# Joint half steps for two pairs of heads, f32 P for two pairs of batch 1, unscaled P in batch 0, and the cap in registers

## The chip, the cores and the metric

One core of one Trainium2 chip runs the whole program. The metric is the device time of one execution in microseconds. Five engines work side by side: TensorE (PE: matmuls, with its weight loads shown apart as PEld), VectorE (DVE), ScalarE (ACT), GpSimd (POOL) and SyncE (SP), which here issues the DMAs.

## The reference

Attention with a soft cap for 4 batches of 12 heads, 448 positions of 64 numbers, then a feed-forward layer with a leaky activation on the 1792 tokens:

```python
scores = scale * q @ k.T                       # (4, 12, 448, 448)
scores = cap * tanh(scores / cap)
attn = exp(scores - max(scores)); attn /= sum(attn) + 1e-9
x = (attn @ v)                                 # heads put side by side: 1792 x 768
h = x @ w_in                                   # 768 x 2048
g = maximum(h, 0) + alpha * minimum(h, 0)
out = g @ w_out                                # 2048 x 768
```

`w_in`, `w_out` and `alpha` come as 64-bit floats, which the kernel makes into f32 with integer operations on DVE.

## The kernel before

Products that must be nearly f32-exact are made in one of two ways: as f32 matmuls (each appears as two instructions in the trace), or as f16 matmuls of operands that were split into a high and a low f16 part, three or four products for one.

**Attention** goes by pairs of heads (6 pairs in a batch). The 448 rows of scores of a head are 3 full blocks of 128 rows and 64 more. `steps` takes two blocks at a time, one of each head: a score product in PSUM, tanh on ACT (`L553`), the row maximum on DVE (`L558`), a small operation that makes the bias of it (`L560`), exp on ACT with the row sums (`L565`), `GUARD` and reciprocal on the sums (`L570`, `L573`). The last 64 rows of both heads stand together in one block of 128 rows, and this half step has half as much to do on every engine but the same number of operations. So a pair takes 4 steps in batches 1 to 3. Batch 0 is cut into two parts of 192 and 256 rows: 2 steps for each pair and part, and of the 192-row part one of the two is a half step.

Then P must be turned (its keys put on partitions). In batch 0, `turn_32` (`L600` to `L616`) makes a diagonal matrix of the row factors 1/sum on ACT or POOL and multiplies each 128x112 piece of the block with it in f32 (`L612`), 4 products for a block, 42 blocks in all; PSUM is copied to `ptall`, and `PV_32` (`L665`) multiplies with the raw f32 v. In batches 1 to 3, `turn_split` scales P by the factors, splits it into f16 parts on ACT, DVE and POOL, and DMAs turn it; `PV_split` (`L651`) takes 24 f16 products for a pair.

Scores of batches 0 and 1 are f32 products of 64x128 tiles (`scores_32`, `L528`). For batches 2 and 3, q and k are scaled and split into `nat`, the two parts of a head side by side on 128 columns and k's parts doubled by a copy (`L768`); one DMA turns 24 groups of 112x128, and a score block is 2 products over 128 rows of the array (`L785`).

**Weights**: DVE converts and splits 16 chunks of w_in and 16 of w_out (`wi`, `wp`); `norms` takes a Gram product on PE and its absolute maximum on DVE (`L370`, 8 times).

**The layer**: `mm1` (`L806`) multiplies w_in with x of a batch, `mm2` (`L847`) w_out with g. The first mm2 needs all of w_out and its scales, and mm1 of batch 1 writes over the g that mm2 of batch 0 reads.

**Order**: every operation is recorded with a priority and a model time per engine (`op`), and `Plan.order` lists them by a simulated run of all queues, choosing the engine where several could do an operation (`either`, `diff`: ACT, DVE, POOL). The result is a fixed order per engine. Until a planned time, PE gets dummy products (`fill`, `L1063`) where it would have nothing to do, so that its clock stays up.

Of the kernel before, what the change touches and what calls it, by code (L numbers as in the profile page):

```python
# [10 lines left out]
F32 = mybir.dt.float32  # L11
# [14 lines left out]
PD_A = 6  # L26
PD_B = 6
MQ = 3
AQ = 3
PEN = 4509.92  # L30
PEN2 = -1345.18
PENP = 6482.25
B0_P = -50.35
LD_P = -35.85
LO_P = 301.38
MM_P = 3324.02
X_P = 53.71
ST_P = 19.81
ST1_P = 13.45
PV_P = 374.14  # L40
QK_P = -32.7
V_P = -1.09
WI_P = 40.03
WI_S = -0.97
A_S = 13.05
MM1_P = 198.89
WO_P = 329.05
WO_S = -16.5
WT_P = -1461.61
WT_S = -141.91  # L50
B1_P = 277.05
B_S = 241.79
EVAC_P = -145.66
# [14 lines left out]
QA = 0.5  # L68
VA = 1.0
FS = [0, 6]  # L70
TURN = 95.0
TURN_P = 905.0
SCORE = 1040.0
# [5 lines left out]
OFF = [34.6, 0.4, 29.9, -6.1, 0.0, 1.5, -90.6, 40.5, 0.0, 0.0, -257.7, 0.0, 2.6, -1.0, 26.8, -8.5, -42.6, 107.4, 10.3, 125.2, 8.6, -267.5, -58.1, 2.0, -9.3, 235.7, 4.8, -32.5, 207.0, 194.2, 463.8, 229.6, 0.0, -31.2, -255.6, -6.9, -24.3, 57.8, -178.1, 70.7, 0.0, 225.2, -115.2, -52.7, 0.0, -130.7, 63.2, 240.7, 63.4, -111.4, 0.0, 0.0, 9.4, 97.8, -60.1, -181.2, -100.1, -35.7, 137.8, 0.0, -6.1, -78.0, -257.2, 31.2, -2.2, -147.9, 21.3, -0.4, 0.0, 21.9, 119.4, -148.7, 89.0, -63.5, 14.5, 76.1, -40.7, -49.1, 31.5, -2.8, 125.9, -8.9, 99.3, -23.6, -83.9, 175.4, 11.7, 163.5, -170.9, 0.0, 13.5, 0.2, -5.3, 0.2, -132.0, -577.9, -1.6, 9.7, -185.1, -10.0, 15.0, -245.3, 0.0, -22.7, 32.7, 149.3, -1091.5, -40.3, 0.0, -672.3, 15.6, -127.9, -897.3, 55.4, -59.5, 0.0, 167.9, 2.2, 12.5, -39.1, 123.8, -60.7, -437.0, -54.8, -543.8, -541.5, 4.4, 0.0, -1.4, -92.4, -0.7, -60.4, 150.0, 75.5, -504.3, 26.7, 69.5, 182.6, -11.4, -57.0, 55.8, 95.6, -4.2, 2.6, 230.8, 0.0, -572.4, 62.6, 1.6, -54.4, 0.0, -3.0, 20.2, 99.9, 396.1, 2.6]  # L79
# [9 lines left out]
class Plan:  # L89
# [16 lines left out]
    def op(self, prio, times, fn, r=(), w=(), rows=1.0, port=True):  # L106
        o = lambda: None
        o.prio, o.times, o.fn, o.rows, o.idx, o.port = prio + OFF[self.tag], times, fn, rows, len(self.ops), port
# [24 lines left out]
    def order(self):  # L133
# [8 lines left out]
        port = {"dve": 0.0, "pool": 0.0}  # L142
# [46 lines left out]
        while todo:  # L189
# [10 lines left out]
            for e in free:  # L200
# [3 lines left out]
                while ready[e]:  # L204
# [20 lines left out]
                    elif e == "pe":  # L225
                        free[e] = run_pe(t, o.rows)
# [36 lines left out]
def kernel(  # L263
# [72 lines left out]
    nat = ct([P, 6 * NCH, P], F16, "nat")  # L336
    qkTs = ct([P, 2, 6 * NCH, CP], F16, "qkTs")
    aux = qkTs[:, 1].rearrange("p g t -> p (g t)").bitcast(F32)
    qzs = [aux[:, :512], aux[:, 512:1024]]
    qzr = [(("qkT", 1), 0, 512), (("qkT", 1), 512, 1024)]  # L340
# [3 lines left out]
    diags = ct([P, 4, P], F32, "diags")  # L344
# [4 lines left out]
    ams = ct([P, 3, 8], F32, "ams")  # L349
    vam = ct([P, 2, 2 * NPAIR], F32, "vam")  # L350
# [17 lines left out]

    def absmax(o, i):
        nc.vector.tensor_reduce(out=o, in_=i, axis=AX.X, op=ALU.max, apply_absolute_value=True)  # L370

# [80 lines left out]
    def vslot(b, pair):  # L452
        n = 2 * NCH * D
        if b == 0 and pair < 3:
            return nat.rearrange("p g t -> p (g t)").bitcast(F32)[:CP, pair * n:(pair + 1) * n], ("nat", pair * n, pair * n + n)
        if b == 0 and pair == 5:
            return xring[:CP, 6:].rearrange("p i e t -> p (i e t)").bitcast(F32)[:, :n], ("x", 12 * S, 12 * S + 2 * n)
        return rvs[:CP, pair % 2], ("rv", pair % 2, pair % 2 + 1)
# [33 lines left out]
    def spans(n, c):  # L492
# [4 lines left out]
        else:  # L497
            for h in range(2):
                yield h, slice(h * QP, (h + 1) * QP), slice(n - QP, n)

    step_no = [0]
    xpos = {}

    def xslot(b, pair):
# [603 lines left out]
```

## Time and profile before

| | us |
|---|---|
| median of 3 runs (lowest, highest) | 695.26 (694.31, 695.97) |
| the profiled execution | 696.31 |
| its span, first to last instruction | 694.5 |
| PE busy | 680.4 |
| DVE busy | 486.9 |
| ACT busy | 420.7 |
| POOL busy | 265.0 |

The span is the time between the first and the last instruction on the engines; 1.8 us of the execution lie around it. Busy shares are means over stages with different limits. Matmuls are pipelined, so the length of a group of PE instructions contains the drain of the last; from the start of one group to the start of the next is what the group takes from the queue.

### The profile page before, as it was taken

What the parts mean: (1) busy time and instruction counts of PE and PEld (TensorE: products, weight loads), DVE (VectorE), ACT (ScalarE), POOL (GpSimd) and SP (SyncE); (2) the same over time, 40 slices, a digit from 0 to 9 for tenths busy, and PEclk for the clock granted to TensorE, in tenths of its full rate; (3) what the DMA queues carried; (4) which work ended last, traced back from release to release, by engine and by line L of the source; (5) the groups of instructions that cost most, each with busy time, mean ns of one, the idle gap of its engine ahead of it and who ended that gap; (6) DMA issues with size and microseconds to landing.
All of it is one profiled execution on the core that took longest, in us unless ns stands there. A gap on an engine that the chain in (4) does not pass through costs nothing.

```text
span 694.5 us, 13601 instructions
## 1 busy us (share of the span) xinstructions
PE 680.4 (98%) x5122; PEld 433.6 (62%) x5122; DVE 486.9 (70%) x953; ACT 420.7 (61%) x828; POOL 265.0 (38%) x405
## 2 busy tenths in 40 slices
PE   8999999999999998999999999999999999999997
PEld 6888887898786555544555555545455555555664
DVE  4899999999989987786886858588688503441000
ACT  5789889777777765773785656477668602331100
POOL 1343366565476662373663524256245200000000
PEclk9999999999999999999999999999999999999999
DMA  9996652975973599867669998596487710000011
GB/s 222 251 324 185 178 196 87 241 151 162 187 158 73 108 195 201 181 112 119 114 119 189 206 181 177 116 159 119 83 159 134 146 33 24 0 1 1 24 40 29
DMA packets 207393, 93.50 MB, mean 135 GB/s; under 512 B 170912, under 2 KB 203616, under 8 KB 207328
## 3 DMA queue, kind: packets, MB, share of 16 engines
q1 hardware_dynamic: 207328, 92.64, 61.9%
q8 instruction: 40, 0.66, 0.4%
q14 instruction: 25, 0.20, 0.1%
HBM read 45.82 MB, written 5.51 MB: 74 GB/s over the span
## 4 chain that ended last, share of the span: by engine, by line
PE 80%; DMA 9%; DVE 5%; ACT 3%; issue 2%; POOL 1%; SPq 1%; ACTq 0%; DVEq 0%; POOLq 0%
PE p L847 29%; PE p L806 24%; PE p L612 6%; DMA ptall<-pw 5%; PE s L785 5%; PE p L651 5%; PE s L528 4%; PE p L665 3%; PE p L490 2%; DMA wp<-in_moe_w_out_dram 2%; PE p L926 1%; DMA qkTs<-nat 1%; DMA nat<-in_v_dram 1%; DVE mxs L558 1%; PE p L390 1%
## 5 line engine op out<-in xcount | busy, mean ns | idle before, releaser
L847 PE MATMUL p<-wp,gall 128*128 128x384 f16 x1344 | 225.7, 326 | 0.0
L806 PE MATMUL p<-xring,wi 128*128 128x448 f16 (+2 forms) x1440 | 225.2, 315 | 0.0
L806 PEld LDWEIGHTS <-wi 128*128 128x128 f16 x1440 | 134.5, 98 | 84.5 <-issue 4.6
L847 PEld LDWEIGHTS <-gall 128*128 128x128 f16 x1344 | 129.7, 98 | 88.5 <-issue 4.1
L565 ACT ACTIVATE tall<-tall,mxs,small 128x448 f32<-128x448 f32 x126 | 94.5, 751 | 23.7 <-POOL mxs L560 14.9
L816 DVE SCALAR_TENSOR_TENSOR gr<-p,ca_g,gr 128x448 f32<-128x448 f32 (+2 forms) x80 | 46.6, 585 | 52.1 <-ACT gr L406 51.9
L558 DVE TENSOR_REDUCE mxs<-tall 128x2 f32<-128x896 f32 x72 | 68.4, 960 | 11.5 <-ACT tall L553 11.2
L406 ACT ACTIVATE gr<-p,cs_g 128x448 f32<-128x448 f32 (+2 forms) x67 | 36.7, 548 | 58.6 <-PE p L806 55.9
L560 POOL TENSOR_SCALAR mxs<-mxs,small 128x2 f32<-128x2 f32 (+1 forms) x68 | 30.4, 448 | 86.9 <-DVE mxs L558 81.3
L570 POOL TENSOR_SCALAR rr<-sums 128x2 f32<-128x2 f32 x96 | 35.2, 367 | 51.8 <-ACT tall L565 35.0
L416 DVE SCALAR_TENSOR_TENSOR pw<-tall,rr,pw 128x448 f16<-128x448 f32 x63 | 46.1, 732 | 6.8 <-ACT pw L406 4.8
L406 ACT ACTIVATE wp<-p,small 128x384 f32<-128x384 f32 x20 | 11.5, 577 | 64.4 <-PE p L847 64.4
L651 PE MATMUL p<-ptall,vs 112*64 112x448 f16 x432 | 45.5, 354 | 1.7 <-DMA ptall<-pw 1.2
L553 ACT ACTIVATE tall<-s,ams 128x896 f32<-128x896 f32 (+1 forms) x48 | 42.3, 901 | 6.1 <-PE s L785 3.5
L413 POOL TENSOR_TENSOR pw<-tall,pw 128x448 f16<-128x448 f32 x35 | 39.8, 1137 | 13.3 <-ACT pw L400 11.0
L400 ACT ACTIVATE gall<-gr 128x384 f16<-128x384 f32 (+4 forms) x55 | 25.4, 467 | 28.2 <-DVE gr L816 27.8
L785 PE MATMUL s<-qkTs 128*128 128x448 f16 (+1 forms) x192 | 38.1, 355 | 2.7 <-ACT tall L553 2.2
L413 POOL TENSOR_TENSOR gall<-gr,gall 128x256 f16<-128x256 f32 (+4 forms) x42 | 33.2, 794 | 13.7 <-ACT gall L400 10.3
L406 ACT ACTIVATE pw<-tall,rr 128x448 f16<-128x448 f32 x43 | 28.5, 663 | 15.6 <-DMA ptall<-pw 11.9
L651 PEld LDWEIGHTS <-vs 112*64 112x64 f16 x432 | 24.3, 110 | 20.7 <-issue 6.0
L612 PE MATMUL p<-diags,gall 128*112 128x128 f32 x280 | 36.0, 278 | 0.5 <-POOL diags L408 0.5
L402 POOL CAST gall<-gr 128x192 f16<-128x192 f32 (+4 forms) x32 | 22.7, 711 | 34.6 <-DVE gr L816 33.9
(155 smaller groups left out, 1000.6 us busy)
## 6 DMA issues: line engine op xcount, KB each, us to landing
wp<-in_moe_w_in_dram SPq DMA_DIRECT2D x16, 768.0 KB, 8.0
wp<-in_moe_w_out_dram SPq DMA_DIRECT2D x16, 768.0 KB, 5.1
rvs<-in_v_dram SPq DMA_DIRECT2D x38, 224.0 KB, 3.5
rqk<-in_q_dram SPq DMA_DIRECT2D x18, 224.0 KB, 3.4
rqk<-in_k_dram SPq DMA_DIRECT2D x18, 224.0 KB, 3.3
ptall<-pw SPq DMA_TRANSPOSE x144, 3.3
wp<-in_k_dram SPq DMA_DIRECT2D x6, 224.0 KB, 9.0
wp<-in_q_dram SPq DMA_DIRECT2D x6, 224.0 KB, 8.0
```

The lines of the kernel that those rows point to most:

```text
L406: nc.scalar.activation(out=o, in_=i, func=AF.Copy, scale=s)
L413: (nc.gpsimd if e == "pool" else nc.vector).tensor_tensor(out=o, in0=a, in1=b, op=ALU.subtract)
L416: nc.vector.scalar_tensor_tensor(out=o, in0=i, scalar=s, in1=hi, op0=ALU.mult, op1=ALU.subtract)
L553: op(pr, {"act": 245 + 377 * m}, lambda e, s=s, t=t, m=m: nc.scalar.activation(out=t, in_=s[:, :m, :S].rearrange("p c (j k) -> p c j k", j ...
L558: op(pr, {"dve": 136 + 469 * m}, lambda e, mt=mt, t=t: nc.vector.tensor_reduce(out=mt, in_=t, axis=AX.XY, op=ALU.max), r=tr, w=[mr], port= ...
L565: nc.scalar.activation(out=t[:, x], in_=t[:, x], func=AF.Exp, scale=capt, bias=mt[:, x:x + 1], accum_out=u.sums[:, c:c + 1])
L612: nc.tensor.matmul(ps_p[h.slot][:CP, j * P:(j + 1) * P], t[:, j], d, start=True, stop=True)
L651: nc.tensor.matmul(pv[x * D:(x + 1) * D, :n], vs[:, z, c:c + D], u.pt[x][:CP, y * NCH + kc], start=(i == 0), stop=(i == len(prods) - 1))
L785: nc.tensor.matmul(s[rows, i, :S], qT[:, x * S + cols.start:x * S + cols.stop], qkT[:, r0:r0 + NCH, :], start=(z == 0), stop=(z == 1))
L806: nc.tensor.matmul(ps_p[h.slot][:, :n], w[:, z, kk, :], x[:, d, o:o + n], start=(kk == 0 and z == d), stop=(kk == NPAIR - 1 and z == 1))
L816: op(pr, {"dve": 198 + 1.07 * n}, lambda e: nc.vector.scalar_tensor_tensor(out=t, in0=ps_p[h.slot][:, :n], scalar=ca_g[:, j:j + 1], in1=t, ...
L847: nc.tensor.matmul(ps_p[h.slot][:, :NH], g[j][:, d, t * P:(t + 1) * P], w[:, z, hf * NH:(hf + 1) * NH], start=(j == 0 and z == d), stop=(j ...
```

## The change

1. **Joint step.** The last 64 rows of two neighbouring pairs of one batch (and part) go in one step of two full blocks: block 0 has head 0 of both pairs, block 1 head 1. Two half steps become one full step, 3 times in batch 0 and 9 times in batches 1 to 3.
2. **Batch 0 unscaled.** P is turned as it comes out of exp by TensorE transposes against the identity, with no diagonal. The factors go into the result: a product of the broadcast factors with the identity (`rows_of`) gives them by columns, scaled by v's factor into SBUF, and `xout_32` multiplies the output of `PV_32` with them before it splits it.
3. **f32 P for two pairs of batch 1** (`FP = [0, 2]`): they take this f32 way in place of the split and the DMAs.
4. **Three f16 products.** Scores of batches 2 and 3 keep the parts of q and k apart, with 64 rows of the array for each head: 3 products for a block in place of 2 products over 128 rows. q and k are split without the doubling copy, all of them on the `direct` path, and the DMA turns 16 groups in place of 24. There are three buffers for it in place of two.
5. **Cap in registers.** exp, and tanh in batches 0 and 1, take their scale from an ACT register in place of a column in SBUF.
6. **Norms on ACT.** `norms` takes the sum of absolute values on ACT, four instructions each, in place of the maximum on DVE.
7. The planner's priorities, offsets and model times are other ones, so the order of all work is new; it now charges 98 ns for a change of the array's tiling. Buffers for v of batch 0 lie elsewhere.

```diff
-PD_A = 6
-PD_B = 6
+NM = 1.0
-QA = 0.5
+QA = 1.0
-TURN = 95.0
-TURN_P = 905.0
-SCORE = 1040.0
+FP = [0, 2]
+TURN = 110.0
+SWITCH = 98.0
+SCORE = (907.0, 957.0)
+SCORE_3 = (580.0, 578.0)
...
+    def bound(e, o, i, func=AF.Abs):
+        if e == "act":
+            nc.scalar.activation(out=junk[:i.shape[0], :i.shape[1]], in_=i, func=func, accum_out=o)
...
+    def scores_3(s, x, u, y, rows, cols):
+        a, q = slice(y * D, (y + 1) * D), u.q
+        for z, w in ((0, 2), (1, 2), (0, 3)):
+            yield lambda z=z, w=w: nc.tensor.matmul(s[rows, x, :S], q[a, z * S + cols.start:z * S + cols.stop], q[a, w * S:(w + 1) * S],
+                                                    start=(z == 0 and w == 2), stop=(w == 3))
...
+        def products(e):
+            for fns in zip(*(u.scores(s, x, *r) for x in range(2) for r in routes[x])):
+                for fn in fns:
+                    fn()
...
+            out=t, in_=s[:, :, :S].rearrange("p c (j k) -> p c j k", j=NCH), func=AF.Tanh, scale=icapr if reg else scale[0]),
...
+                nc.scalar.activation(out=t[:, x], in_=t[:, x], func=AF.Exp, scale=capr,
+                                     bias=mt[:, x:x + 1], accum_out=sums[:, u.idx % 3, col + x:col + x + 1])
...
+    def units(us, n, st_p, finish):
+        nf, m = 2 * (n // P), n % P
+        for i, u in enumerate(us):
+            for c in range(0, nf, 2):
+                cols = slice(c // 2 * P, c // 2 * P + P)
+                step(u, u.prio + st_p * c, c, [[(u, y, slice(0, P), cols)] for y in range(2)], u.scale)
+            later, z = [], nf
+            if m and i == 0:
+                tail = slice(n - m, n)
+                z += 2
+                later = step(u, u.prio + st_p * nf, nf, [[(v, y, slice(x * QP, (x + 1) * QP), tail) for x, v in enumerate(us)] for y in range(2)], u.joint)
+            if not u.dma:
+                factors(u, u.prio + st_p * nf, 0, z)
+            finish(u)
...
-        d, dr = diags[:, i], ("dg", i, i + 1)
-        op(pr, either(P, f=True, pool=True), lambda e: scaled(e, d, ident, f), r=[identr, fr], w=[dr])
...
-                nc.tensor.matmul(ps_p[h.slot][:CP, j * P:(j + 1) * P], t[:, j], d, start=True, stop=True)
+                nc.tensor.transpose(ps_p[h.slot][:CP, j * P:(j + 1) * P], t[:, j], ident)
...
+        def rows_of(e):
+            for i, c, y, rows, cols in u.facts:
+                nc.tensor.matmul(ps_p[h.slot][y * D:(y + 1) * D, cols], rr[:, i, c:c + 1].to_broadcast([P, D]), ident[:, rows], start=True, stop=True)
...
+        op(prio, either(n, True, f=True), lambda e: scaled(e, R, ps_p[h.slot][:, :n], vb[u.b].s), r=[h, (vb[u.b].tok, 7, 9)], w=[rt], port=False)
...
+    def xout_32(u, prio, h, n, o):
+        op(prio, {"dve": 160 + 1.04 * n}, lambda e: nc.vector.tensor_tensor(out=t, in0=ps_p[h.slot][:, :n], in1=R, op=ALU.mult),
+        op(prio, either(n, pool=True), lambda e: copy(e, hi, t), r=[tt], w=[xr(u.b, u.pair, 0, o, n)])
+        op(prio, diff(n, False), lambda e: minus(e, lo, t, hi), r=[tt, xr(u.b, u.pair, 0, o, n)], w=[xr(u.b, u.pair, 1, o, n)])
...
-            both = nat[:CP, 2 * NCH:]
-            op(pr, {"dve": 420}, lambda e: nc.vector.tensor_copy(both[:, :, D:], both[:, :, 0:D]), w=[nt[1], nt[2]])
...
+    capr, icapr = (nc.scalar.alloc_register(x) for x in ("capr", "icapr"))
+    nc.scalar.load(capr, capt[:1].bitcast(I32))
+    nc.scalar.load(icapr, icap[:1].bitcast(I32))
```

## Rows read from the trace of the kernel before

**Rows 1.** The page: busy time with share and instructions; granted clock in 40 slices.
```profile
PE 680.4 (98%) x5122; PEld 433.6 (62%) x5122; DVE 486.9 (70%) x953; ACT 420.7 (61%) x828; POOL 265.0 (38%) x405
...
PEclk9999999999999999999999999999999999999999
```

**Rows 2.** Windows: length, busy PE, PEld, DVE, ACT, POOL, clock, DMA share, GB/s.
```profile
40.00:80.00 40.00, 40.00 (x428) 33.20 (x426) 39.66 (x70) 35.58 (x76) 17.33 (x28) 1.00 0.86 258
...
200.00:240.00 40.00, 38.37 (x341) 25.98 (x337) 38.76 (x69) 31.49 (x52) 26.33 (x31) 1.00 0.44 80
...
360.00:400.00 40.00, 40.00 (x260) 22.71 (x255) 30.92 (x65) 25.67 (x50) 18.29 (x30) 1.00 0.98 187
...
640.00:694.50 54.50, 50.10 (x309) 29.94 (x306) 0.00 (x0) 4.64 (x8) 0.00 (x0) 0.99 0.11 29
```

**Rows 3.** Timeline of PE before mm2: start, length, instructions, idle before them.
```profile
211.58 3.02 PE L1063 MATMUL p<-ident 128*128 128x128 f16 x51
216.05 1.05 PE L1063 MATMUL p<-ident 128*128 128x128 f16 x16 [1.46 <-DVE xring L416]
216.94 2.11 PE L847 MATMUL p<-wp,gall 128*128 128x384 f16 x12
```

**Rows 4.** PE groups by form: busy in all, mean ns of one, idle before.
```profile
L651 PE MATMUL p<-ptall,vs 112*64 112x448 f16 x432 | 45.5, 354 | 1.7 <-DMA ptall<-pw 1.2 <-issue 0.4
L612 PE MATMUL p<-diags,gall 128*112 128x128 f32 x280 | 36.0, 278 | 0.5 <-POOL diags L408 0.5
...
L1063 PE MATMUL p<-ident 128*128 128x128 f16 x136 | 10.7, 241 | 3.1 <-DVE xring L416 1.5 <-POOL ident masks.py:199 1.4 <-DVE gr L816 0.2
...
L387 PE MATMUL p<-ident,n_wi 128*4 128x128 f32 x4 | 1.1, 272 | 0.0
```

**Rows 5.** Timeline of PE, one block of P turned.
```profile
59.16 1.13 PE L612 MATMUL p<-diags,gall 128*112 128x128 f32 x8
60.22 0.80 PE L490 MATMUL p<-ident,wp 112*64 112x112 f32 x12
```

**Rows 6.** Timeline of PE, f32 scores: a half step, later a full step.
```profile
144.18 0.97 PE L528 MATMUL s<-qkTs 64*64 64x224 f32 x8
145.08 1.66 PE L806 MATMUL p<-xring,wi 128*128 128x192 f16 x18
...
199.32 1.03 PE L528 MATMUL s<-qkTs 64*128 64x224 f32 x8
200.28 0.52 PE L926 MATMUL p<-wp 128*128 128x128 bf16 x6
```

**Rows 7.** Timeline of PE, f16 scores: a full step and a half step.
```profile
530.08 0.92 PE L785 MATMUL s<-qkTs 128*128 128x448 f16 x4
530.84 2.11 PE L847 MATMUL p<-wp,gall 128*128 128x384 f16 x12
...
540.25 0.57 PE L785 MATMUL s<-qkTs 128*64 128x448 f16 x4
540.75 4.08 PE L847 MATMUL p<-wp,gall 128*128 128x384 f16 x24
```

**Rows 8.** Timeline of PE, P times V in f32 for 192 rows.
```profile
50.72 1.52 PE L665 MATMUL p<-ptall,rvs 112*64 112x192 f32 x16
52.17 1.13 PE L612 MATMUL p<-diags,ptall 128*112 128x128 f32 x8
```

**Rows 9.** ACT groups by form, columns as in rows 4.
```profile
L406 ACT ACTIVATE pw<-tall,rr 128x448 f16<-128x448 f32 x43 | 28.5, 663 | 15.6 <-DMA ptall<-pw 11.9 <-DVE rr L573 2.2 <-DVE wp L902 1.1
...
L565 ACT ACTIVATION_READ_ACCUMULATOR tall<-tall,mxs,small 128x1 f32 x126 | 23.6, 187 | 0.0
...
L400 ACT ACTIVATE pw<-tall 128x448 f16<-128x448 f32 x37 | 21.2, 574 | 14.4 <-DMA ptall<-pw 11.9 <-POOL tall L408 1.5 <-DVE pw L413 0.7
```

**Rows 10.** DVE groups by form, columns as in rows 4.
```profile
L416 DVE SCALAR_TENSOR_TENSOR pw<-tall,rr,pw 128x448 f16<-128x448 f32 x63 | 46.1, 732 | 6.8 <-ACT pw L406 4.8 <-POOL pw L408 1.7
...
L370 DVE TENSOR_REDUCE n_wi<-p 128x4 f32<-128x512 f32 x8 | 5.4, 680 | 0.1
```

## What I expect, and why

> **What bounds the kernel now.** I began with the busy times. PE is busy for 680.4 us of a span of 694.5 and its granted clock is full in every slice [rows 1], so the first guess is that the time is the sum of what stands in PE's queue. The windows show where that holds [rows 2]: from 360 to 400 us PE has no idle time while DVE works 30.9 of 40 us and ACT 25.7. There, only fewer PE nanoseconds help. From 40 to 80 us PE is full too, but DVE works 39.66 of 40 us. That early stage has two limits at once. Which of them ends last is seen where it closes, just ahead of the first mm2 [rows 3]: from 211.58 us PE runs 51 and then 16 dummy products with 1.46 us of idle between them, and mm2 begins at 216.94. So PE had about 5.4 us to spare, and the conversion of w_out on the other engines, DVE above all (38.76 of 40 us from 200 to 240), sets that start. After it PE sets everything. The last window holds 4.4 us of idle in the tail, which the change doesn't touch [rows 2].
>
> I therefore make the sum in two stages, before 217 us (PE's sum and DVE's both have to shrink) and after it (PE's sum alone). For PE I take the distance from the start of a group to the start of the next one.
>
> **The change, part by part, on PE.**
>
> *Turning in batch 0.* One block takes 60.22 − 59.16 = 1.06 us [rows 5], with 8 instructions. The new form has 4 instructions for a block. Transposes of 128 f32 columns are in the trace: one instruction each, 272 ns against the 278 ns of one of the two instructions of a product [rows 4]. So a transpose costs one of the two passes. Half of 1.06 is 0.53; I take 0.55. The bounds are 0.45 (half of a block with no drain between) and 1.06 (no gain). 42 blocks × 0.51 = −21, and since neighbouring blocks overlap already I count −19.7.
>
> *The factors by columns.* P times V for 192 rows takes 52.17 − 50.72 = 1.45 us for 16 instructions [rows 8]. `rows_of` streams the same columns once where that does so four times: 0.36 us, with the start of a group about 0.4; for 256 rows about 0.5. 6 × 0.4 + 6 × 0.5 = +5.4. Below that it can't go much; with no overlap of the two column halves it would be double, +10.
>
> *f32 P for two pairs of batch 1.* Removed: one f16 P times V, 45.5 us / 18 = 2.5 us [rows 4]. Added: 7 blocks × 0.5 = 3.5; factors 0.85; the f32 product of 448 rows, 1.45 × 448/192 = 3.4, less its fixed part 3.15. That is +5.0 for a pair, +10 for two.
>
> *Joint f32 steps.* A half step takes 145.08 − 144.18 = 0.90 us, a full one 200.28 − 199.32 = 0.96 [rows 6]. Half steps have 64x64 tiles, two at once; a joint step has twice as many on four tiles. If all four go at once it costs a full step plus a little, 1.0, and saves 0.8; if only two go at once, 1.8, and it saves nothing. The full step proves overlap in the rows of the array (8 instructions of 224 f32 columns in 0.96 us) and the half step on both sides; I take 1.0. 6 × 0.8 = −5.
>
> *f16 scores of batches 2 and 3.* A full step is 0.76 us for 4 products of 448 columns, a half step with two column tiles 0.50 for 4 [rows 7]. So two column tiles give (0.76/2 = 0.38) plus 0.12 for the change of tiling. The new full step has 6 products on two row tiles: 3 × 0.19 + 0.12 = 0.69, and the joint step the same on four tiles. Two pairs: before 6 × 0.76 + 2 × 0.50 = 5.56, after 7 × 0.69 = 4.83; 6 such couples give −4.4. The other end: f16 products on row tiles stand nowhere in the trace, and if they didn't overlap a step would be 6 × 0.19 + 0.12 = 1.26, 7 × 1.26 = 8.8, which is +19.5. I take the f32 steps as the nearest row, where row tiles do overlap.
>
> The Trainium skill speaks against this part: "TensorEngine Tiling (Array Packing)", section "Key Properties", says that a change of the tiling mode drains TensorE, and the old full steps had the tiling of their neighbours. The 0.12 us above [rows 7] agrees with such a drain; it is in the sum.
>
> Sum on PE: −19.7 + 5.4 + 10 − 5 − 4.4 = **−13.7 us**. Of it, −4.5 − 19.7 + 5.4 + 10 = −8.8 lies before mm2 and −4.9 behind (with the last f32 step).
>
> **The other engines before 217 us.** Norms leave DVE: 8 × 0.68 = −5.4 [rows 10]. They put 32 instructions on ACT, each with a read of the accumulator of 187 ns and fewer columns than the 574 ns of a 448-column copy [rows 9]: between 6 and 24 us, I take 15. The register for the scale: the same pass with a column as scale takes 663 ns and without one 574 [rows 9], so 0.09 us; 70 exps (42 blocks of batch 0, 28 of four pairs of batch 1) and some 36 tanhs before mm2 give −9.5 on ACT if a register costs nothing, 0 if it costs as much as the column. The split of 14 blocks of P goes: half of them had a 732 ns DVE pass [rows 10], −5.1, with as much again in ACT's and POOL's passes; PSUM copies of the same blocks come back on ACT or DVE. The 42 diagonals leave ACT and POOL. `xout_32` adds one DVE pass of 192 or 256 columns for 12 units and 2 longer ones, and its subtraction may go to POOL: 0 to +6. So DVE alone loses 5 to 11 us, ACT stays about even, POOL, with 17 to 26 of 40 us busy [rows 2], gets room to take work from DVE. I count mm2's start as 11 us earlier. PE could follow: 8.8 less to do and the 5.4 of spare time. Less is queued on SP (fewer P and q/k turns), and nothing new waits behind a DMA. The joint step adds a wait: the first pair's last 64 rows wait for the second pair's q and k, and behind it on PE stands P times V of the first pair. mm1 and mm2 products hide it, as they do now; without that cover it would be one load and turn for each couple. The register loads stand ahead of ACT's first copy, which waits for q and k anyway: I take 0.
>
> **Forecast.** 11 before mm2, 5 behind it, and some 1.5 of the small idles there (1.63 us in the window from 200 us [rows 2] is of their size), as turns have fewer DMAs to wait for: −17.5. From the profiled 696.3 that is 678.8; the median lies 1.05 lower than that execution, so **678**.
>
> **The rivals.**
> *mm2's start doesn't move.* If the norms on ACT and the register eat what DVE gains, or the new order doesn't use POOL's room, PE's 8.8 us turn into dummies ahead of mm2 and only the 5 behind it and the idles are left: 696.3 − 6.5 = 690, 689 by the median. For it: DVE is full from 40 us on [rows 2]. Against: 5.4 us leave DVE with certainty. Chance 0.22.
> *PE's spare time goes too.* If DVE's stage shrinks by 15 or more, all of −13.7, 5.4 and most of the other dummies (10.7 in all [rows 4]) go: 696.3 − 24 = 672, 671 by the median. Chance 0.14.
> *Slower: row tiles don't overlap in f16.* Place: the 42 steps of batches 2 and 3, where PE has no slack. Price: +19.5 there in place of −4.4. With the gain before mm2 that is 696.3 − 11 − 0.5 + 19.5 = 704, 703 by the median. It turns the whole change at a step of about 1.07 us, where the 42 steps (33.4 us now) cost the 11.5 more that the rest gains. Against it: the f32 steps. Chance 0.07.
> *Clock.* The transposes now stand in the stage where PE also waits most. If stretches with them didn't keep the clock, PE's work there would take twice as long: half of the 40 us of a window like 40 to 80 [rows 2] in two such windows is +40, some 718. The granted clock is full there now, with f32 products and dummies in between [rows 1, 4]. Chance 0.03. By the Trainium skill, "TensorE: Matmul & The Clock Gate", "Part 4: PE-mode transpose", transposes don't count as busy the way products do; no run here has enough of them to show it.
> *The register saves nothing.* ACT then has 9.5 more in the first stage, and mm2 starts about 3 us later: 681, inside the forecast's own case.
>
> **How the numbers follow.** Forecast (673 to 685) 0.54, the two others of the same sign 0.22 and 0.14, slower ones 0.10. The range leaves out the slower cases and the tail of the best one: 663 to 692. A measurement of this kernel tells some 0.2% (1.4 us) from no change. Of the 0.22, 0.04 may end within that. So faster 0.86, same 0.04, slower 0.10.
>
> **What would show it.** L612's successor: 4 instructions for a block and about half a microsecond. f16 score steps of 0.65 to 0.75 us with 6 products, joint steps the same with 12. The first mm2 at about 206 us, with fewer dummies ahead of it. exp at about 660 ns. PE's busy time at 655 to 670 us and the clock full throughout. A prediction gone wrong would show as dummies or idle time ahead of mm2, or score steps above 1 us.

## The result, and the profile after

| | before | after |
|---|---|---|
| median (lowest, highest), us | 695.62 (694.31, 696.48) | 685.99 (681.80, 686.89) |
| the profiled execution | 696.31 | 686.12 |
| its span | 694.5 | 684.3 |

Four runs of each stand behind the medians. The ratio is 0.9851, with an interval from 0.9808 to 0.9895: shorter by 9.6 us where I had forecast 17.3. The sign was right and the time lies in the stated range; 8 us of the forecast gain didn't come. The shares and the chain on the page of the changed kernel:

```profile
PE 666.8 (97%) x5151; PEld 413.4 (60%) x5151; DVE 481.7 (70%) x922; ACT 395.4 (58%) x853; POOL 237.4 (35%) x354
...
PE 66%; DVE 19%; DMA 6%; ACT 3%; SPq 3%; issue 2%; POOL 1%; ACTq 0%; DVEq 0%; POOLq 0%
```

PE is still busy for 97% of the span, DVE and ACT each work less than before [rows 1]. But the chain that ended last has changed its make-up: on the page of before PE had 80% of it and DVE 5%, and now PE has 66% and DVE 19%. So more of the time is decided by the other engines, DVE above all. The windows by stage say where. Columns are the length, then busy PE, PEld, DVE, ACT, POOL, then clock, DMA share, GB/s. First the kernel before, cut at the same places:

```profile
40.00:160.00 120.00, 119.64 (x1275) 100.81 (x1273) 116.72 (x210) 99.92 (x213) 64.73 (x96) 1.00 0.66 184
160.00:240.00 80.00, 77.79 (x740) 58.16 (x738) 76.35 (x136) 59.58 (x109) 46.90 (x59) 1.00 0.67 140
240.00:560.00 320.00, 316.03 (x1957) 170.77 (x1957) 240.23 (x480) 208.99 (x408) 142.04 (x221) 1.00 0.80 151
```

and the changed kernel:

```profile
40.00:160.00 120.00, 112.51 (x1183) 85.29 (x1180) 112.88 (x188) 96.48 (x247) 58.30 (x66) 0.97 0.58 177
160.00:240.00 80.00, 79.17 (x726) 62.01 (x724) 73.72 (x131) 54.00 (x120) 50.40 (x63) 1.00 0.58 117
240.00:560.00 320.00, 318.04 (x2081) 168.66 (x2081) 240.85 (x479) 191.30 (x381) 120.10 (x200) 1.00 0.72 138
```

PE's idle time is the length less its busy time. From 40 to 160 us it was 0.36 us and is 7.49. From 160 to 240 it went from 2.21 to 0.83, from 240 to 560 from 3.97 to 1.96. And in that first stage the clock is 0.97 and not full. The timeline of PE around the first mm2 (start, length, instructions, in brackets the idle time before them) answers [rows 3]:

```profile
219.87 2.14 PE L886 MATMUL p<-xring,wi 128*128 128x256 f16 x18
222.17 2.12 PE L927 MATMUL p<-wp,gall 128*128 128x384 f16 x12 [0.16 <-DVE gr L896]
```

The dummies ahead of mm2 are gone, and what is left of waiting is 0.16 us. But mm2 begins at 222.17 us and not at my 206: PE arrives with real work up to the last moment. Two of PE's groups by form (busy time in all and mean ns of one; idle time before them):

```profile
L665 PE MATMUL p<-ident,gall 128*112 128x128 f32 x136 | 19.6, 278 | 2.5 <-ACT qkTs L421 1.8 <-ACT ptall L421 0.7
...
L1149 PE MATMUL p<-ident 128*128 128x128 f16 x69 | 6.7, 263 | 1.4 <-POOL ident masks.py:199 1.4
```

69 dummies are left of 136 [rows 4], all of them before 38 us, and a group of the transposes has the largest idle time of any group ahead of it, up to the end of ACT's copies.

**The 10.2 us of span, accounted for.** Dummies: 10.7 − 6.7 = 4.0 gained. Idle: 694.5 − 680.4 = 14.1 before, 684.3 − 666.8 = 17.5 after, 3.4 lost. The clock: 4 us at 0.62 and 4 us at 0.95 make 1.72 us lost, and there are two such places (near 66 and 148 us), 3.4 lost. What remains is PE's real work: 666.8 − 6.7 − 3.4 = 656.7 against 680.4 − 10.7 = 669.7, 13.0 gained. And −4.0 + 3.4 + 3.4 − 13.0 = −10.2. So the work was priced well (13.7 forecast). The rest was not.

### The profile page after: what moved, and what is told of

It is laid out like the page before. It is cut to its first block, busy times and chain, and to the rows that moved or that the text cites. A ratio compares the mean times of both kernels' runs of the same rounds, so it can differ in the third digit from the quotient of the medians.

```text
span 684.3 us, 13548 instructions
## 1 busy us (share of the span) xinstructions
PE 666.8 (97%) x5151; PEld 413.4 (60%) x5151; DVE 481.7 (70%) x922; ACT 395.4 (58%) x853; POOL 237.4 (35%) x354
## 4 chain that ended last, share of the span: by engine, by line
PE 66%; DVE 19%; DMA 6%; ACT 3%; SPq 3%; issue 2%; POOL 1%; ACTq 0%; DVEq 0%; POOLq 0%
PE p L886 27%; PE p L927 24%; PE p L711 4%; DVE mxs L583 4%; PE s L557 3%; DMA ptall<-pw 3%; PE p L738 2%; DVE wp L437 2%; PE s L551 2%; SPq L454 1%; DVE wi L437 1%; DVE wp L992 1%; DVE wp L986 1%; PE p L515 1%; SPq L847 1%
## 5 line engine op out<-in xcount | busy, mean ns | idle before, releaser
L590 ACT ACTIVATE tall<-tall,mxs 128x448 f32<-128x448 f32 x126 | 82.7, 659 | 15.1 <-POOL mxs L585 9.8
L585 POOL TENSOR_SCALAR mxs<-mxs,small 128x2 f32<-128x2 f32 x62 | 33.3, 537 | 99.1 <-DVE mxs L583 69.3
L583 DVE TENSOR_REDUCE mxs<-tall 128x2 f32<-128x896 f32 x63 | 66.9, 1075 | 1.0 <-ACT tall L579 0.9
L434 POOL TENSOR_TENSOR gall<-gr,gall 128x192 f16<-128x192 f32 (+4 forms) x52 | 45.0, 869 | 33.0 <-ACT gall L421 21.7
L437 DVE SCALAR_TENSOR_TENSOR pw<-tall,rr,pw 128x448 f16<-128x448 f32 x56 | 41.1, 735 | 14.1 <-ACT pw L427 12.4
L579 ACT ACTIVATE tall<-s,ams 128x896 f32<-128x896 f32 x42 | 41.1, 1000 | 14.6 <-PE s L557 6.0
L421 ACT ACTIVATE gall<-gr 128x384 f16<-128x384 f32 (+4 forms) x51 | 24.2, 477 | 30.7 <-DVE gr L896 30.6
L711 PE MATMUL p<-ptall,vs 112*64 112x448 f16 x384 | 40.3, 355 | 0.2 <-issue 0.2
L607 POOL TENSOR_SCALAR rr<-sums 128x2 f32<-128x2 f32 (+2 forms) x70 | 27.6, 394 | 29.5 <-ACT tall L590 22.3
L427 ACT ACTIVATE pw<-tall,rr 128x448 f16<-128x448 f32 x27 | 17.9, 665 | 27.2 <-DMA ptall<-pw 23.2
L711 PEld LDWEIGHTS <-vs 112*64 112x64 f16 x384 | 21.2, 110 | 17.3 <-issue 3.7
L434 DVE TENSOR_TENSOR gall<-gr,gall 128x384 f16<-128x384 f32 (+4 forms) x60 | 28.4, 478 | 4.1 <-ACT gall L421 1.6
L421 ACT ACTIVATE ptall<-p 112x512 f32<-112x512 f32 (+1 forms) x48 | 26.3, 580 | 6.5 <-PE p L665 5.3
L421 ACT ACTIVATE pw<-tall 128x448 f16<-128x448 f32 x37 | 21.2, 574 | 14.5 <-DMA ptall<-pw 12.6
```

The lines of the kernel that those rows point to most:

```text
L421: nc.scalar.activation(out=o, in_=i, func=AF.Copy)
L427: nc.scalar.activation(out=o, in_=i, func=AF.Copy, scale=s)
L434: (nc.gpsimd if e == "pool" else nc.vector).tensor_tensor(out=o, in0=a, in1=b, op=ALU.subtract)
L437: nc.vector.scalar_tensor_tensor(out=o, in0=i, scalar=s, in1=hi, op0=ALU.mult, op1=ALU.subtract)
L579: op(pr, {"act": (152 if reg else 245) + 377 * 2}, lambda e: nc.scalar.activation(out=t, in_=s[:, :, :S].rearrange("p c (j k) -> p c j k", ...
L583: op(pr, {"dve": 136 + 469 * 2}, lambda e: nc.vector.tensor_reduce(out=mt, in_=t, axis=AX.XY, op=ALU.max), r=tr, w=[mr], port=False)
```

## The experiments

The question was why PE, with 13 us less to do, now waits in a stage where it had no idle time. Two theories. **Load**: DVE, working 39 of 40 us from 80 to 160 us, or ACT, with the norms added, can't deliver faster; take work from them and the waits go. DVE was full in this stage before the change too; PE was only later then. **Order**: the fixed order lets PE reach certain copies out of PSUM before they are made, each at the end of a chain (row maximum, bias, exp, copy) that stands in one queue behind other things; a lighter load moves the chain little, and another order would make the wait go. More work on PE ahead of such a copy would make the wait go by either theory. Unless a heading says otherwise, an edit is one of the changed kernel and keeps its order.

### The changed kernel again

The first thing to know is how far it repeats. No edit.

> The changed kernel as it is, once more, beside the next ones on one chip. The earlier call had the column for the scales at 681.8 us, where the changed kernel had 686 in an earlier call. If registers really cost time in this order (exps that end earlier meet other operations on the port of VectorE and GpSimd), this run is at 685 to 687 and the profile has the wait of TensorE at 64 us. If that was only the difference between two calls, it is at 681 to 683.

Median 683.39 us (681.31 to 686.10), ratio 0.9833 (0.9799 to 0.9867). That lies between the two ranges, and its profile has the wait at 64 us all the same; what registers do is left to the runs further below. In this second profile PE's idle time from 40 to 160 us is 6.50 us:

```profile
40.00:160.00 120.00, 113.50 (x1217) 87.45 (x1214) 114.34 (x193) 97.44 (x250) 60.88 (x68) 0.99 0.60 184
```

With the first four, ten runs lie between 681.3 and 686.9, a spread of 5.6 us. The 17 runs of before beside these six span 2.5 but for one at 700.92. Part of the spread has a visible cause. The wait that PE has longest in the first profile of the changed kernel (in all, times, longest):

```profile
PE p L665 <- ACT qkTs L421: 1.8, 1, 1.8
```

It ends at 65.61 us. Windows of the changed kernel around it:

```profile
64.00:66.00 2.00, 0.39 (x4) 0.39 (x4) 0.18 (x1) 2.00 (x7) 1.03 (x2) 1.00 0.45 80
66.00:70.00 4.00, 4.00 (x29) 2.58 (x29) 3.12 (x5) 2.08 (x6) 2.23 (x1) 0.62 0.46 156
```

The same in the second profile of the same kernel:

```profile
64.00:66.00 2.00, 0.28 (x3) 0.28 (x4) 0.18 (x1) 2.00 (x6) 1.10 (x2) 1.00 0.44 77
66.00:70.00 4.00, 3.99 (x38) 2.85 (x37) 3.02 (x5) 2.16 (x6) 2.12 (x1) 1.00 0.46 158
```

PE works 0.39 of 2 us in the one and 0.28 in the other, and then the granted clock is 0.62 over 4 us in the one and full in the other. The P times V product that stands there, in the first profile:

```profile
67.35 3.44 PE L738 MATMUL p<-ptall,rvs 112*64 112x256 f32 x16
70.72 0.65 PE L665 MATMUL p<-ident,ptall 128*112 128x128 f32 x4
```

and in the second, from the wait on:

```profile
65.72 0.65 PE L665 MATMUL p<-ident,gall 128*112 128x128 f32 x4 [1.77 <-ACT qkTs L421]
...
67.45 1.98 PE L738 MATMUL p<-ptall,rvs 112*64 112x256 f32 x16
69.36 0.65 PE L665 MATMUL p<-ident,ptall 128*112 128x128 f32 x4
```

70.72 − 67.35 = 3.37 us against 69.36 − 67.45 = 1.91. Twice the 1.91 would be 3.82: most of the 16 instructions ran at the lower of the two levels, 1.2 of 2.4 GHz. So a wait of 1.8 us with a nearly idle PE ahead of it is followed by the lower clock in some executions and not in others. The first profile has two such falls (0.61 from 148 to 152 us), the second has one (0.62 from 144 to 148), at about 1.7 us each.

### What the longest wait hangs on: the bias on DVE

```diff
-lambda e: (nc.gpsimd if e == "pool" else nc.vector).tensor_scalar(
+lambda e: (nc.gpsimd if e == "pool" and u.idx >= 18 else nc.vector).tensor_scalar(
     out=mt, in0=mt, scalar1=ncap, scalar2=EXP_BIAS, op0=ALU.mult, op1=ALU.add), w=[mr])
```

The chain of the 1.75 us wait can be read backwards in the timeline of the changed kernel, all engines, other lines left out:

```profile
60.15 3.70 POOL L585 TENSOR_SCALAR mxs<-mxs,small 128x2 f32<-128x2 f32 x1
...
62.84 0.95 DVE L992 SCALAR_TENSOR_TENSOR wi<-wp,wi 128x768 int32<-128x768 int32 x1
...
63.88 0.67 ACT L590 ACTIVATE gall<-gall,mxs 128x448 f32<-128x448 f32 x1 [2.55 <-POOL mxs L585]
...
65.20 0.36 ACT L421 ACTIVATE qkTs<-p 128x256 f32<-128x256 f32 x1
...
65.61 0.65 PE L665 MATMUL p<-ident,gall 128*112 128x128 f32 x4 [1.75 <-ACT qkTs L421]
```

PE waits for a copy on ACT (L421) that stands behind two exps (L590). The first of these waits 2.55 us for the bias of the row maxima, and that operation on POOL, for 2 columns, takes 3.70 us where the mean of its group is 537 ns. DVE runs nearly back to back through those 3.70 us, and POOL ends 0.06 us after DVE's run ends at 63.79. So the edit puts this small operation on DVE for the first 18 units.

> The changed kernel in its own order, but the small operation that makes exp's bias runs on VectorE in batches 0 and 1 where the order has it on GpSimd. Theory (a small GpSimd operation that comes late holds up exp, then ScalarE's copies, then TensorE, whose clock falls after the wait): the waits of TensorE at 64 us (1.75 us) and 113 us go, at least one of the two falls of the granted clock goes, and the time is 3 to 5 us shorter, 681 to 683. Rival (VectorE is the limit of the first 160 us and any operation added to it costs its length): some 25 operations of 0.25 us make it 2 to 6 us longer, 688 to 692.

Median 684.67 us (683.62 to 685.08), ratio 0.9856 (0.9839 to 0.9872), in neither range. Its windows:

```profile
40.00:80.00 40.00, 39.73 (x448) 31.86 (x447) 38.80 (x71) 34.02 (x87) 17.32 (x15) 1.00 0.71 215
80.00:120.00 40.00, 36.80 (x374) 28.61 (x372) 39.86 (x78) 35.32 (x90) 14.82 (x17) 1.00 0.55 172
120.00:160.00 40.00, 36.59 (x421) 26.94 (x418) 39.49 (x70) 29.78 (x77) 12.29 (x16) 1.00 0.54 171
```

and the last two for the changed kernel:

```profile
80.00:120.00 40.00, 36.87 (x374) 28.39 (x371) 38.92 (x68) 34.23 (x93) 22.10 (x27) 1.00 0.63 191
120.00:160.00 40.00, 37.40 (x401) 27.06 (x400) 39.46 (x65) 31.36 (x78) 13.67 (x19) 0.96 0.45 143
```

The long wait is gone: PE works 39.73 us from 40 to 80 where it was 38.24. The wait at 113 us, which I had named too, is gone as well. But from 80 to 160 PE has 3.20 and 3.41 us of idle time where it had 3.13 and 2.60, DVE is fuller, and the time isn't shown to differ. The late POOL operation was the cause of one wait and not of the loss.

### Less load on ACT: no norms

```diff
-op(prio, {"act": 500}, lambda e, i=i: bound(e, n[:, i:i + 1], ...),
+op(prio, {"act": 500}, lambda e: None,
...
+nc.gpsimd.memset(n_wi, 6.0)
```

It leaves out the sums of absolute values; a constant stands for them.

> The changed kernel in its own order without the 32 norm instructions on ScalarE (their result is a constant, so this part of the computation is left out). Theory of ScalarE as the late engine: with 15 us less on it the copies that TensorE waits for come earlier, the waits of 0.7 to 1.1 us between 100 and 150 us go, and the time is 4 to 7 us shorter. Rival (ScalarE has room, the late copies come from VectorE or GpSimd ahead of them): less than 1.5 us.

Median 684.38 us (681.37 to 686.93), ratio 0.9852 (0.9813 to 0.9891). In its profile ACT works 91.1 of the 120 us from 40 to 160 where it was 96.5, and PE has 7.89 us of idle time there, no less than the 7.49. One wait of 0.8 us, for the norms themselves, goes, and one of 1.0 us for a copy on DVE comes; the other longest waits, of 1.8, 1.1 and 1.1 us, stay. ACT's added load isn't the cause of the loss.

### Less load on DVE

```diff
-to_f32(prio, WO_STAGE[j], room[j], room_r(j), share(j, XO))
+to_f32(prio, WO_STAGE[j], room[j], room_r(j), share(j, XO), False)
```

It leaves out the pass that puts the sign into w_out, 16 operations of 0.95 us on DVE, whose busy time falls by 11.9 us.

> The changed kernel in its own order without one of the three VectorE passes that convert a chunk of w_out (the sign of w_out, so that part of the computation is left out): 16 passes of 0.95 us, 15 us less on VectorE between some 90 and 220 us. If VectorE sets the end of that stage, TensorE's waits from 100 to 150 us shrink and the time is 5 to 10 us shorter, 676 to 681. If ScalarE's copies do, or TensorE itself, less than 2 us.

Median 681.67 us (678.95 to 682.28), ratio 0.9791 (0.9759 to 0.9824). Its windows from 80 us on:

```profile
80.00:120.00 40.00, 36.85 (x372) 28.57 (x372) 38.89 (x69) 34.77 (x90) 20.26 (x26) 1.00 0.57 177
120.00:160.00 40.00, 37.87 (x440) 28.59 (x439) 32.88 (x57) 30.57 (x80) 14.47 (x22) 1.00 0.56 177
```

From 120 to 160 us DVE works 32.88 us, 7 fewer, and PE still has 2.13 us of idle time there, where the two profiles of the changed kernel have 2.60 and 1.59. So a full DVE isn't what makes the waits of this stretch. The median is 1.7 us below the kernel run again, with intervals that overlap.

From 80 to 120 us the run says nothing of the kind. The passes that it leaves out stand from 122 us on; before that DVE works 38.89 of 40 us as it did, and PE's idle time is 3.15 us beside 3.13. And there the chain that ended last in the changed kernel goes through DVE alone, one operation behind the other for 29 us, but for 0.9 us in which the engine waited for nothing that the profile shows (start, length):

```profile
81.13 0.42 DVE xs L748
...
109.35 1.00 DVE mxs L583
...
110.44 2.24 POOL mxs L585
```

The maxima that exp waits for (`L583`) stand in that queue among the conversions of the weights. Whether fewer operations on DVE or another order of the same ones would end these waits is open: no run takes work from DVE in this stretch.

### Both, and shorter copies

```diff
-v.pv[y][:, :, cols],  ps_p[...].rearrange(...)[:, :,  i * k_:(i + 1) * k_]
+v.pv[y][:, :1, cols], ps_p[...].rearrange(...)[:, :1, i * k_:(i + 1) * k_]
```

Two kernels: the bias on DVE together with no sign pass, and, as shown, the copies of the f32 P out of PSUM a quarter as wide. The second leaves out three quarters of P (the buffer is set to zero at the start).

> The changed kernel in its own order, with the bias operation of batches 0 and 1 on VectorE in place of GpSimd and without the sign pass of w_out on VectorE (that part of the computation is left out). Each alone left TensorE's waits between 40 and 160 us at 5 to 7 us. Theory A (VectorE's load and GpSimd's late small operations limit together, so that either one takes over when the other goes): the waits shrink to under 3 us and the time is 676 to 679. Theory B (the order itself: TensorE stands behind copies out of PSUM that are queued on ScalarE behind exps, whatever the loads are): the waits stay at 5 us or more and the time is 679 to 682.

> The changed kernel in its own order, with the copies of the turned P out of PSUM a quarter as wide (three quarters of P are zero in batch 0 and the two f32 pairs, so that part of the computation is left out): 56 blocks, 20 to 25 us less on ScalarE and VectorE, all in the operations that TensorE is seen to wait for. If the length of these copies is what TensorE waits for, its waits between 40 and 160 us go to under 3 us and the time is 677 to 680. If what is queued ahead of them is, they stay above 4 us and the time is 680 to 683.

The first: 680.33 us (679.17 to 681.17), ratio 0.9805 (0.9792 to 0.9819). The second: 681.62 us (680.55 to 682.48), ratio 0.9823 (0.9810 to 0.9837). Their windows, in this order:

```profile
40.00:160.00 120.00, 114.39 (x1257) 89.34 (x1254) 112.30 (x209) 99.65 (x255) 44.13 (x49) 1.00 0.62 192
40.00:160.00 120.00, 114.27 (x1239) 89.04 (x1235) 113.94 (x195) 87.42 (x250) 65.14 (x69) 0.99 0.62 189
```

PE's idle time is 5.61 us in the one and 5.73 in the other, where the two profiles of the changed kernel have 7.49 and 6.50. So 1 to 2 us of the waits go, whether DVE loses 16 operations and the late one on POOL is moved, or the very copies that PE waits for are cut to a quarter (12.1 us less on ACT, where I had put 20 to 25 on ACT and DVE together). The load on ACT, the length of the copies and the load on DVE from 120 us on are no main cause. For DVE from 80 to 120 us that isn't shown: the first kernel has it busy for 39.83 of 40 us there, and 3.19 of its 5.61 us stand there.

### More work on PE: products in place of transposes

```diff
-nc.tensor.transpose(ps_p[h.slot][:CP, j * P:(j + 1) * P], t[:, j], ident)
+nc.tensor.matmul(ps_p[h.slot][:CP, j * P:(j + 1) * P], t[:, j], ident, start=True, stop=True)
```

The same result by a product with the identity, at the price of the old turn: two instructions for one.

> The changed kernel in its own order, but the 224 transposes of P are f32 products with the identity, 8 instructions for a block and not 4: 56 x 0.45 to 0.5 = 25 to 28 us more on TensorE before 160 us. If TensorE is near its limit there, as the prediction has it, the time is longer by that less its waits and dummies there (13 us), 12 to 22 us: 695 to 706. If the stage waits for other engines anyway, less than 8. The granted clock: if transposes don't hold it up, it stays at full here and the two falls go; if the waits let it fall, they go as well only where the waits do.

Median 697.86 us (697.50 to 698.30), ratio 1.0056 (1.0041 to 1.0072). Its windows:

```profile
40.00:160.00 120.00, 119.28 (x1267) 99.10 (x1266) 102.06 (x167) 92.03 (x227) 45.50 (x60) 1.00 0.52 164
```

The idle time from 40 to 160 us is 0.72 us, the clock is full, and DVE is emptier (102.06 of 120). With more to do PE comes late enough for every copy. That fits both theories, and doesn't tell order from load: it shows that the waits hang on PE's own pace. PE's busy time is 686.7 − 665.3 = 21.4 us longer than in the kernel run again, and 23.1 with the 1.7 us that the lower clock took there. The span grew by 695.7 − 681.5 = 14.2 us, so 9 of the 23.1 us filled what had been waits and lower clock. Read the other way round: transposes alone return about 60% of what they save. And in this order, with everything but the transposes, the changed kernel is a little slower than the kernel before.

What it doesn't tell is which link of the chain (the maximum, the exp, a place in ACT's queue) binds each wait. An order planned anew would, and none with the waits alone removed was made.

### Registers: put into the kernel before, and taken out of the changed one

```diff
-nc.scalar.activation(out=t[:, x], in_=t[:, x], func=AF.Exp, scale=capt, ...)
+nc.scalar.activation(out=t[:, x], in_=t[:, x], func=AF.Exp, scale=capr, ...)
```

This is the edit of the kernel before, with the two registers loaded at the start and tanh changed alike; the edit of the changed kernel is its reverse.

> The kernel before in its own order with the scales of exp and tanh from registers. ScalarE loses some 15 us of 421. By the prediction's reading (PE and VectorE end last before mm2, PE alone behind it) the time moves by less than 1.5 us, 694 to 696. If ScalarE held up VectorE before mm2, up to 4 us shorter.

> The changed kernel in its own order with the scales of exp and tanh from a column in SBUF again. exp takes 0.75 us in place of 0.66. If ScalarE is the late engine before mm2, its 10 us there cost 3 to 6 us, 689 to 692. If ScalarE has room, less than 1.5 us.

The kernel before with registers: 693.37 us (692.93 to 700.48), ratio 0.9989 (0.9967 to 1.0011). The changed kernel without them: 681.81 us (681.32 to 683.60), ratio 0.9819 (0.9799 to 0.9839), beside 0.9833 for the kernel as it is. The group of exps on ACT in the first of these kernels:

```profile
L565 ACT ACTIVATE tall<-tall,mxs 128x448 f32<-128x448 f32 x126 | 82.9, 659 | 21.9 <-POOL mxs L560 14.9 <-DVE mxs L560 6.6 <-DVE s_wo L1009 0.2
```

It was 751 ns before, so a register takes 92 ns off each, as costed. The Trainium skill gives the same price for a pointer operand beside an immediate ("ScalarE: Activation LUTs", section "What ACT_TABLE_LOAD costs": each pointer operand adds about 93 ns); the trace agrees on the size, and no run here has an exp with an immediate beside it. ACT works 404.0 us in place of 420.7, and no time is shown to come of it in either kernel: PE doesn't wait for ACT by ACT's load.

### Columns and the bias on DVE together

The edits of two of the runs above in one kernel.

> The changed kernel in its own order with the scales from columns and the bias operation of batches 0 and 1 on VectorE, both at once. If each takes away the same wait at 64 us, the two together give what one gives, 681 to 684. If they act on different waits, 678 to 680. If VectorE ends last from 80 to 160 us, the bias operations there give some back, 683 to 685.

Median 688.19 us (686.92 to 690.04), ratio 0.9893 (0.9861 to 0.9924). That is above all three ranges, and more than either edit alone (681.81 and 684.67). In its profile 4.94 us of idle time stand between 240 and 560 us, where the changed kernel has 1.96. Why, I can't say; it stays open. It is a warning about how such edits add up in a fixed order.

### Three f16 products in the kernel before

```diff
-for i, c in enumerate(blocks):
-    for z in range(2):
-        ...
+for z, w in ((0, 2), (1, 2), (0, 3)):
+    for i, c in enumerate(blocks):
+        ...
+        nc.tensor.matmul(s[rows, i, :S], qT[a, z * S + cols.start:z * S + cols.stop], qT[a, w * S:(w + 1) * S], ...)
```

The operands are read where the old layout has other values, so the scores aren't the reference's; the work on PE is that of three products. So it puts the rival that row tiles don't overlap to the test by itself.

> The kernel before in its own order, with only the score products of batches 2 and 3 changed to three products on 64 rows of the array (the operands are read where the old layout has other parts, so the scores of these batches are not the reference's; everything else is done as before). A full step should go from 0.76 us to about 0.65, a half step from 0.50 to about 0.69: 36 x -0.11 + 12 x 0.19 = -1.7 us. TensorE alone sets the time there, so the time should move by that much, 692.5 to 693.5. Rival (no overlap of the row halves in f16): a step of 1.26 us, 18 us more, 713.

Median 696.89 us (695.78 to 703.83), ratio 1.0034 (1.0009 to 1.0059). Two steps in the timeline of PE, a full one and a half one:

```profile
529.08 0.74 PE L785 MATMUL s<-qkTs 64*128 64x448 f16 x6
529.75 2.12 PE L847 MATMUL p<-wp,gall 128*128 128x384 f16 x12
...
539.22 0.76 PE L785 MATMUL s<-qkTs 64*64 64x448 f16 x6
539.90 1.31 PE L847 MATMUL p<-wp,gall 128*128 128x384 f16 x7
```

529.75 − 529.08 = 0.67 us for 6 products, against 0.76 for 4 [rows 7]: the row tiles overlap, and the rival is refuted. The half step takes 0.68 where it took 0.50. For a pair that is 3 × 0.09 − 0.18 = 0.09 us gained, 1 us in all; PE's busy time didn't move (680.7) and its idle time from 240 to 560 us went from 3.97 to 5.05. So without the joint step the three products bring nothing, and the time got a little longer, where I had expected it 1.7 us shorter by PE's sum. Where the idle time comes from wasn't followed.

### No f32 P in batch 1

```diff
-FP = [0, 2]
+FP = [0, 0]
```

Here the planner lists another order, by the same priorities.

> The changed kernel without part 3: the two pairs of batch 1 split P in f16 and turn it by DMA as the others. The order is planned anew by the same planner with the same priorities. By the prediction's prices TensorE has 10 us less and VectorE 5 us more, with as much on ScalarE and GpSimd. If TensorE's sum decides, 674 to 678; if the other engines before mm2 decide, 684 to 690.

Median 704.39 us (703.47 to 705.82), ratio 1.0155 (1.0139 to 1.0172). Its dummies:

```profile
L1149 PE MATMUL p<-ident 128*128 128x128 f16 x713 | 45.4, 223 | 1.4 <-POOL ident masks.py:199 1.4
```

PE's real work is 688.3 − 45.4 = 642.9 us, 13.8 less than the changed kernel's 656.7 (I had put the two pairs at 10), and the time is some 18 to 21 us longer, outside both ranges: 36.6 us of dummies stand between 160 and 240 us, and mm2 begins at 233.5. So with two more pairs split PE waits for the other engines or the transposes by DMA ahead of mm2; which of them wasn't followed. The part that costs PE most holds the change up, in the orders that this planner makes. How much of the difference is the new order and not the work, this run can't say.

## Why the forecast was right in sign, and 8 us too low

The prices first. The steps in PE's timeline of the changed kernel, each from its start to the next line's start:

```profile
59.98 0.65 PE L665 MATMUL p<-ident,gall 128*112 128x128 f32 x4
60.56 0.80 PE L515 MATMUL p<-ident,wp 112*64 112x112 f32 x12
...
132.31 3.23 PE L738 MATMUL p<-ptall,rvs 112*64 112x448 f32 x16
135.47 0.52 PE L1006 MATMUL p<-wp 128*128 128x128 bf16 x6
...
208.04 0.99 PE L551 MATMUL s<-qkTs 64*64 64x224 f32 x16
208.96 2.14 PE L886 MATMUL p<-xring,wi 128*128 128x256 f16 x18
...
459.58 0.74 PE L557 MATMUL s<-qkTs 64*128 64x448 f16 x6
460.25 0.26 PE L408 MATMUL p<-ident,small 112*2 112x112 f32 x1
...
480.38 1.44 PE L557 MATMUL s<-qkTs 64*64 64x448 f16 x18
481.75 3.58 PE L886 MATMUL p<-xring,wi 128*128 128x448 f16 x18
```

and on ACT, the groups by form:

```profile
L590 ACT ACTIVATE tall<-tall,mxs 128x448 f32<-128x448 f32 x126 | 82.7, 659 | 15.1 <-POOL mxs L585 9.8 <-DVE mxs L585 5.0 <-DVE s_wo L1095 0.2
...
L389 ACT ACTIVATE junk<-p 128x128 uint8<-128x128 f32 x32 | 8.7, 271 | 0.7 <-PE p L1006 0.5
...
L389 ACT ACTIVATION_READ_ACCUMULATOR junk<-p 128x1 f32 x32 | 6.4, 200 | 0.0
```

| step | forecast | measured |
|---|---|---|
| a block turned, us | 0.55 | 0.58 |
| f32 P times V for 448 rows | 3.15 | 3.16 |
| joint f32 step | 1.0 | 0.92 |
| f16 full step, 6 products | 0.69 | 0.67 |
| f16 joint step, 12 products (in the line of 18, less a full step) | 0.69 | 1.37 − 0.67 = 0.70 |
| real work on PE in all | −13.7 | −13.0 |
| exp, ns | 660 | 659 |
| norms on ACT, us | 15 | 8.7 + 6.4 = 15.1 |
| DVE before 240 us | −5 to −11 | 219.5 to 213.7 = −5.8 |
| dummies and idle time | −3.8 | −4.0 + 3.4 = −0.6 |
| clock | 0 | +3.4 |
| first mm2, us | 206 | 222.2 (219.6 the second time) |

**Right**: nearly every price of an operation, by start-to-start times of rows that already stood in the profile of before (the factors by columns for 256 rows took 0.59 us where I had 0.5). The chosen values lay near the right end where the bounds were far apart, above all the f16 row tiles, priced by the f32 steps [rows 6, 7]. What I had put in for the change of tiling came out as the half step had shown: 0.67 us is three times 0.19 plus 0.10.

**The mis-sized term** is dummies and idle time, with the clock behind it. The step that failed stands in the first part: "From 40 to 80 us PE is full too, but DVE works 39.66 of 40 us", which I took as a stage with two limits of which mm2's start was the end [rows 2, 3]. I then let PE follow by 11 us, with no new idle time. A PE without idle time in that stage was not at the limit of its neighbours by a margin I had measured; it was only later than they were. Once it had 13 us less to do it caught up with them: 7.49 us of idle time in place of 0.36, and the longest wait was followed by a lower clock. From 40 to 160 us DVE itself had lost only 116.72 − 112.88 = 3.84 us, where I had let the whole stage end 11 us earlier ("PE could follow"). The runs with less work clear ACT's load, the length of the copies and DVE's load from 120 us on. What binds PE from 80 to 120 us, where 3.13 of the 7.49 us stand, DVE's load or its order, stays open; that the order makes the waits behind 120 us is argued, as what is left, and no run changes the order alone.

**mm2's start** failed for another reason as well: I summed PE's work before mm2 as if the same work stood there. Of the f32 score products 376 of 384 now stand before mm2, where 328 stood, that is 6 steps of 0.96 us; and P times V of four pairs of batch 1 where there were three. So about 8 us of batch 1's work moved ahead of mm2, and what follows mm2 became shorter: 694.5 − 216.9 = 477.6 us before, 684.3 − 222.2 = 462.1 after. The start of mm2 was no measure of the gain in an order planned anew. That the sum of a stage which was to end 11 us earlier and ended 5 us later still came out inside the range is owed to the price of the work on PE, and in part to luck.

**The rivals.** *mm2's start doesn't move* came true by its letter (and by its time, 689, it lay 3 us off, where the forecast lay 8 off), but not by its mechanism: the saved work didn't turn into dummies. *PE's spare time goes too* came true for the 4.0 us of dummies ahead of mm2, and was lost elsewhere. That row tiles don't overlap was refuted. *The register saves nothing* is half right: it saves 92 ns an exp and no time. *Clock* happened in small: two falls of 1.7 us in one profile and one in the next, where I had put 40 us at a chance of 0.03. I had asked whether transposes keep the clock up. With the same transposes in the same order, the granted clock is 1.00 from 40 to 160 us in the profiles with the bias on DVE, without norms and without the sign pass, so transposes in this number, among other products, don't by themselves bring it down. Whether they count less than products, as the Trainium skill has it ("TensorE: Matmul & The Clock Gate", "Part 4: PE-mode transpose"), no run here shows. Nor do waits alone decide, since the 1.77 us wait above was followed by a full clock. No run here has the waits without the transposes, so the two aren't told apart.

No complete version is shown to be better than the changed kernel: the one without registers has the lowest median, 681.81, and its interval overlaps that of the kernel run again.

## What to carry to other kernels

Priced by start-to-start times, PE's work can be forecast to about a microsecond; what can't be read from busy shares is whether its neighbours could keep up if it were faster, so an engine with no idle time says nothing of the margin behind it: the lead of the copies it reads, ready so long before their use, would say it. In an order fixed ahead, time saved on one engine comes back only in part (here about 60% for the transposes alone). Less load on the others brought back at most 1 to 2 us of the waits; before calling load cleared by such a run, look whether the lighter engine is still full in the stretch in question, and whether the chain that ended last runs through it there. And when a plan is made anew, sum the work before a landmark by counting what stands there, not by assuming it is the old list.

## What the runs showed of the hardware

- A GpSimd operation on 2 columns took 3.70 us while DVE ran nearly back to back with operations most of which read two tiles, where the mean of its group is 537 ns. The Trainium skill ("SBUF — State Buffer", section "SBUF: two separate sides") tells of a port pair that a DVE operation of certain kinds or a GpSimd operation holds for a whole instruction while the other waits. The trace agrees as far as it shows POOL done 0.06 us after DVE's run, of several instructions and not one; that the port was what it waited for is not shown.
- After a wait in which PE worked 0.3 to 0.4 of 2 us, the granted clock was 0.62 over the next 4 us in one execution and 1.00 in another of the same kernel.
- Four 64x64 tiles of f32 products at once: 16 instructions in 0.92 us, against 0.90 us for 8 with two tiles [rows 6]. The joint step gave the whole of its saving.
